# Batch 0 transposed on TensorE, its pairs scored in another order, split work in pieces, one plus three PSUM banks

## The chip, the cores and the metric

One core of a Trainium2 chip. The metric is device time in microseconds (us), median over runs. Most runs of one kernel lie within one per cent, but some lie higher: a run more than 1.5% above the fastest run of its kernel is called slow, and all comparisons here use the other, fast, runs. Ratios are the mean time of one kernel's fast runs over that of the other's fast runs of the same rounds on the same chip, so they are not quite the ratio of the medians that are quoted.

## The reference, cut to what matters

```python
def _attn_ref(q, k, v, proj):          # q, k, v: 4 batches, 8 heads, 768 rows, 64 columns
    q_bucket = bits_to_int(q @ proj > 0)      # 6 hash bits a row
    k_bucket = bits_to_int(k @ proj > 0)
    scores = where(q_bucket == k_bucket, scale * q @ k.T, -1e9)
    return softmax(scores) @ v

x = attention output as 3072 rows of 512
h = maximum(maximum(x @ w1, x @ w2), x @ w3)  # 512 -> 768
out = h @ w_out                               # 768 -> 512
```

## The kernel before

Heads are worked on in pairs, four pairs to a batch. To prepare a pair, q and k are split in two fp16 parts on VectorE (four instructions: `split_h` and `split_r` for each), transposed, and hashed: TensorE multiplies by the projection, VectorE compares and writes six rows of ±32768 under the 64 data rows, so that the score matmul masks by itself. A score unit is two score matmuls, one exp on ScalarE, and, two units later, six matmuls with v ("attend"). There are 192 units. When a half of a batch (four pairs) is done, its FFN is cut in atoms and strewn among the later units.

PSUM is the memory in which TensorE leaves its results; `bufs` is the number of buffers of a pool there. To evacuate a result is to copy it out, and until then its buffer is taken.

```python
sc_ps = ... bufs=2   # scores, two banks each
av_ps = ... bufs=2   # attend results
mm_ps = ... bufs=2   # all else: transposes, hash, mean of v, xT, FFN

def xbar(n, b, pr):  # the transpose by DMA
    nc.sync.dma_start_transpose(T[n, b, pr][:], S16[n, b, pr]...)

# batch 0: pairs 0 and 1 transposed on TensorE, 2 and 3 by DMA; splits partly on GpSimd
def prep(b, pr, s, lead, lag):          # batches 1 to 3; s is a unit
    at(s - lead, lambda: [load(n, b, pr, nc.gpsimd) for n in "qkv"])
    def split():
        operands(b, pr)
        for n in "qk":
            split_h(n, b, pr, nc.vector)
            split_r(n, b, pr)
            xbar(n, b, pr)
    at(s, split)
    at(s + 2, lambda: vcast(b, pr))
    at(s + lag, lambda: hash_half(b, pr, 0))
    at(s + lag + 1, lambda: hash_half(b, pr, 1))
    at(s + lag + 1, lambda: hash_rows(b, pr))
    at(s + lag + 2, lambda: meanv(b, pr))

for b in range(1, B):
    for pr in range(NP):
        if b == 1: prep(b, pr, 32 + 6 * pr, 10, 9)
        else:      prep(b, pr, 2 * (b - 1) * NUG + 14 + 10 * pr, 10, 10)

for u in range(N + LAG + 4):            # program order of every engine
    if u < N: score(u)
    if LAG <= u < N + LAG: attend(u - LAG)
    for fn in todo.pop(u, []): fn()
    ...                                 # FFN atoms, 0.64 us of them a unit
```

All engines take their instructions in this program order. (... marks cuts.)

The softmax here doesn't subtract the row's maximum and nothing guards it: scores larger than these inputs give would overflow.

## Time and profile before

| | before |
|---|---|
| time, median | 362.04 us (361.45 to 362.47, 3 runs) |
| TensorE (PE) busy | 292.0 us of a span of 359.8 |
| VectorE (DVE) busy | 202.2 us |
| ScalarE (ACT) busy | 197.3 us |
| mean granted TensorE clock | 0.915 |

The prediction below shows the lines. One slip in it has to be known first: its four dated exps are not units 41, 62, 150 and 191 but, counted from unit 0, units 45, 61, 152 and 191. These are units 41, 62 and 150 in the timeline of the kernel before (start, length, engine, line, operation, shapes, and in brackets the idle time before it and what ended it):

```profile
93.93 0.90 ACT L245 ACTIVATE AT<-sc,bias_t 128x768 f16<-128x768 f32 x1 [0.22 <-PE sc L241]
135.27 0.90 ACT L245 ACTIVATE AT<-sc,bias_t 128x768 f16<-128x768 f32 x1 [1.88 <-PE sc L241]
280.68 0.92 ACT L245 ACTIVATE AT<-sc,bias_t 128x768 f16<-128x768 f32 x1
```

### The profile page before, as it was taken

What the parts mean: (1) busy time and instruction counts of PE and PEld (TensorE: products, weight loads), DVE (VectorE), ACT (ScalarE), POOL (GpSimd) and SP (SyncE); (2) the same over time, 40 slices, a digit from 0 to 9 for tenths busy, and PEclk for the clock granted to TensorE, in tenths of its full rate; (3) what the DMA queues carried; (4) which work ended last, traced back from release to release, by engine and by line L of the source; (5) the groups of instructions that cost most, each with busy time, mean ns of one, the idle gap of its engine ahead of it and who ended that gap; (6) DMA issues with size and microseconds to landing.
All of it is one profiled execution on the core that took longest, in us unless ns stands there. A gap on an engine that the chain in (4) does not pass through costs nothing.

```text
span 359.8 us, 6801 instructions
## 1 busy us (share of the span) xinstructions
PE 292.0 (81%) x2752; PEld 178.2 (50%) x2752; DVE 202.2 (56%) x407; ACT 197.3 (55%) x257; POOL 80.5 (22%) x97
## 2 busy tenths in 40 slices
PE   1475709988769887987978896987978899999995
PEld 1253405655435454554644464554645466666552
DVE  2569504267578667577574655577575544444542
ACT  2346414866336355764664674764665587888221
POOL 1963220544160004404040012404010000010000
PEclk9999555589889899999898998999899999999999
DMA  7545998719955707666237108466224000200202
GB/s 257 189 112 101 132 127 136 262 26 197 214 120 165 118 3 189 192 146 177 46 89 161 58 3 219 162 147 174 49 39 108 31 1 2 89 2 1 89 0 87
DMA packets 58191, 39.76 MB, mean 111 GB/s; under 512 B 45360, under 2 KB 51888, under 8 KB 58160
## 3 DMA queue, kind: packets, MB, share of 16 engines
q1 hardware_dynamic: 49280, 20.06, 25.9%
q0 software_dynamic: 8432, 18.88, 21.4%
q8 instruction: 21, 0.34, 0.4%
q10 hardware_dynamic: 448, 0.40, 0.3%
q14 instruction: 10, 0.08, 0.1%
HBM read 25.17 MB, written 6.29 MB: 87 GB/s over the span
## 4 chain that ended last, share of the span: by engine, by line
PE 62%; DVE 24%; DMA 8%; issue 4%; ACT 1%; ACTq 0%; DVEq 0%
PE ps L306 24%; PE sc L241 15%; PE av L261 8%; PE po L318 8%; DMA kT<-ks 6%; DVE qs L148 4%; PE hps L174 4%; DVE ht L313 3%; DVE hb L179 3%; DVE ks L142 2%; DVE qT L183 2%; DVE qs L142 2%; DMA k<-in_k_dram 2%; DVE kT L183 2%; DVE ks L148 2%
## 5 line engine op out<-in xcount | busy, mean ns | idle before, releaser
L245 ACT ACTIVATE AT<-sc,bias_t 128x768 f16<-128x768 f32 x192 | 171.5, 903 | 103.4 <-PE sc L241 102.0
L306 PE MATMUL ps<-xT,w_sb 128*128 128x384 f16 x576 | 121.3, 337 | 14.0 <-DVE ht L313 12.2
L241 PE MATMUL sc<-qT,kT 70*128 70x384 f16 x384 | 104.3, 356 | 4.4 <-DVE qT L183 1.8
L313 DVE TENSOR_TENSOR ht<-ht,ps 128x384 f16<-128x384 f16 x96 | 52.6, 548 | 73.2 <-PE ps L306 72.0
L261 PEld LDWEIGHTS <-AT 128*128 128x128 f16 x1152 | 66.1, 103 | 31.4 <-issue 9.3
L282 POOL TENSOR_TENSOR xn<-t,rr 128x384 f16<-128x384 f32 x24 | 20.8, 868 | 242.4 <-PE sc L241 139.0
L306 PEld LDWEIGHTS <-w_sb 128*128 128x128 f16 x576 | 50.4, 100 | 46.8 <-issue 26.8
L261 PE MATMUL av<-vone,AT 128*128 128x65 f16 x1152 | 71.4, 200 | 0.0
L241 PEld LDWEIGHTS <-kT 70*128 70x128 f16 x384 | 37.5, 105 | 32.5 <-issue 8.1
L311 ACT CAST ht<-ps 128x384 f16<-128x384 f32 x48 | 22.8, 475 | 33.2 <-PE ps L306 33.2
L318 PE MATMUL po<-wout_sb,ht 128*128 128x512 f16 x144 | 36.4, 395 | 2.7 <-DVE hb L179 2.5
L179 DVE TENSOR_SCALAR hb<-hps 128x384 f16<-128x384 f32 x32 | 17.7, 554 | 34.3 <-PE hps L174 34.2
L174 PE MATMUL hps<-kT,PA 128*32 128x384 f16 x64 | 12.3, 377 | 15.7 <-DMA kT<-ks 10.1
L324 DVE COPY osb<-po 128x512 f32<-128x512 f32 x16 | 11.0, 690 | 21.3 <-PE po L318 21.3
L318 PEld LDWEIGHTS <-ht 128*128 128x128 f16 x144 | 13.3, 101 | 17.5 <-issue 6.3
L277 DVE TENSOR_TENSOR t<-av,mv 128x390 f32<-128x390 f32 x32 | 18.0, 561 | 6.1 <-PE av L261 5.8
L174 PE MATMUL hps<-qT,PA 128*32 128x384 f16 x64 | 13.2, 378 | 7.5 <-DVE xT L293 4.2
L292 PE MATMUL xps<-iden,xn 128*128 128x128 f16 x96 | 11.5, 234 | 9.2 <-DVE ht L313 9.2
L213 POOL CAST vone<-v 128x768 f16<-128x768 f32 x16 | 16.6, 1042 | 6.5 <-DMA v<-in_v_dram 6.3
L148 DVE SCALAR_TENSOR_TENSOR qs<-q,qs 128x768 f16<-128x768 f32 (+1 forms) x17 | 17.5, 1031 | 0.5
L148 DVE SCALAR_TENSOR_TENSOR ks<-k,ks 128x768 f16<-128x768 f32 (+1 forms) x17 | 17.0, 998 | 0.5
L174 PEld LDWEIGHTS <-PA 128*32 128x32 f16 x128 | 4.1, 95 | 25.9 <-issue 18.1
(47 smaller groups left out, 195.8 us busy)
## 6 DMA issues: line engine op xcount, KB each, us to landing
v<-in_v_dram POOLq DMA_DIRECT2D x16, 384.0 KB, 5.1
out_dram<-osb SPq DMA_DIRECT2D x24, 256.0 KB, 2.0
q<-in_q_dram POOLq DMA_DIRECT2D x12, 384.0 KB, 3.7
k<-in_k_dram POOLq DMA_DIRECT2D x12, 384.0 KB, 4.8
w_sb<-in_moe_w_dram POOLq DMA_DIRECT2D x6, 384.0 KB, 11.6
q<-in_q_dram SPq DMA_DIRECT2D x3, 384.0 KB, 5.8
k<-in_k_dram SPq DMA_DIRECT2D x3, 384.0 KB, 7.5
wout_sb<-in_moe_w_out_dram POOLq DMA_DIRECT2D x1, 768.0 KB, 15.2
```

What stands on the lines that cost most here:

```text
L148: nc.vector.scalar_tensor_tensor(out=s[:, a, D : 2 * D], in0=x32, scalar=QS, in1=s[:, a, 0:D], op0=AluOp.mult, op1=AluOp.subtract)
L174: nc.tensor.matmul(hps[32 * g : 32 * (g + 1), 0:HQ], w[:], t[:, a : a + CH, :], start=s, stop=not s)
L179: nc.vector.tensor_scalar(out=out, in0=hps[:, 0:HQ], scalar1=0.0, scalar2=0.5, op0=AluOp.is_gt, op1=AluOp.subtract)
L241: nc.tensor.matmul(sc[:, i, 0:HQ], kT[0:KR, hh * NCH + 2 * j + i, :], qT[0:KR, hh * NCH + hf * CH : hh * NCH + (hf + 1) * CH, :], start=Tr ...
L245: nc.scalar.activation(AT[:], sc[:, :, 0:HQ], ActFn.Exp, bias=bias_t[:], scale=EXP_SCALE)
L261: nc.tensor.matmul(av[:, o : o + D + 1], AT[:, i, c * P : (c + 1) * P], vones[b % 2][:, 2 * pr + hh, 2 * j + i, 0 : D + 1], start=first, s ...
L277: nc.vector.tensor_tensor(out=t[:, :, :, 0 : D + 1], in0=av[:, :, :, 0 : D + 1], in1=mvs[b, pr][:].unsqueeze(2).to_broadcast([P, 2, CH, D ...
L282: eng.tensor_tensor(out=xv, in0=t[:, :, :, 0:D], in1=rr[:].to_broadcast([P, 2, CH, D]), op=AluOp.mult)
L306: nc.tensor.matmul(ps[:, 0:HQ], w_sb[i][:, jc, fb * P : (fb + 1) * P], xT[:, jc, :], start=jc == 0, stop=jc == NJ - 1)
L311: nc.scalar.copy(ht[:], ps[:, 0:HQ])
L313: nc.vector.tensor_tensor(out=hts[fb][:], in0=hts[fb][:], in1=ps[:, 0:HQ], op=AluOp.max)
L318: nc.tensor.matmul(ps[:], hts[fb][:, c * P : (c + 1) * P], wout_sb[:, fb, :], start=fb == 0, stop=fb == NF - 1)
```

## The change

Its intent: take the DMA transposes out of batch 0, where TensorE stood for them, and let each pair's preparation hide behind more score work; cut the split block on VectorE into pieces, so that it holds up nothing for long; give the shared work three banks.

```diff
-    av_ps = ... bufs=2      mm_ps = ... bufs=2
+    av_ps = ... bufs=1      mm_ps = ... bufs=3
+    nc.scalar.dma_start(p32[:], proj[:, :])          # now ahead of the first k load
     load("q", 0, 0, nc.sync, (0, 1))
     load("k", 0, 0, nc.scalar, (0, 1))
 ...
-    units = [... for b in range(B) for hf in range(2) for pr in range(NP) ...]
+    blocks = [(0, hf, pr) for pr, hf in ((0, 0), (0, 1), (1, 0), (1, 1), (2, 0), (3, 0), (2, 1), (3, 1))]
+    blocks += [(b, hf, pr) for b in range(1, B) for hf in range(2) for pr in range(NP)]
 ...
+    def front(b, pr, s):                              # pairs 1 to 3 of batch 0
+        at(s, split_h q); at(s, split_r q); at(s + 1, split_h k); at(s + 1, split_r k)
+        ...  four TensorE transposes at s + 3 and s + 4, evacuated by VectorE
+        tail(b, pr, s + 5)
+    def tail(b, pr, s):                               # the hash work
+        at(s, hash_half 0); at(s + 1, hash_half 1); at(s + 2, rows of head 0); at(s + 3, rows of head 1)
 ...
     def prep(b, pr, s, lead, lag):
-        at(s, split)                                  # all four at once
+        for i, n in enumerate("qk"):
+            at(s + 2 * i, lambda n=n: split_h(n, b, pr, nc.vector))
+            at(s + 2 * i + 1, lambda n=n: split_r(n, b, pr))
+            at(s + 2 * i + 1, lambda n=n: xbar(n, b, pr))
+        at(s + 4, lambda: vcast(b, pr))
+        tail(b, pr, s + lag)
+        at(s + lag + 4, lambda: meanv(b, pr), 0.34)
-            if b == 1: prep(b, pr, 32 + 6 * pr, 10, 9)
-            else:      prep(b, pr, 2 * (b - 1) * NUG + 14 + 10 * pr, 10, 10)
+            if b == 1: prep(b, pr, 26 + 7 * pr, 7, 12)
+            else:      prep(b, pr, 2 * (b - 1) * NUG + 6 + 12 * pr, 10, 12)
 ...  FFN atoms begin at unit 41, at an even rate to the end; the first attend of a block goes behind them
```

Left out here: the loads of batch 0 move from the queues of GpSimd and ScalarE to that of SyncE, all but one; GpSimd loses its four splits of batch 0, and ScalarE three of its four evacuations.

More of the change, by code (lines that the diff above doesn't have):

```diff
@@ L60 @@
     sc_ps = ctx.enter_context(tc.tile_pool(name="sc_ps", bufs=2, space=bass.MemoryType.PSUM))
-    av_ps = ctx.enter_context(tc.tile_pool(name="av_ps", bufs=2, space=bass.MemoryType.PSUM))
-    mm_ps = ctx.enter_context(tc.tile_pool(name="mm_ps", bufs=2, space=bass.MemoryType.PSUM))
+    av_ps = ctx.enter_context(tc.tile_pool(name="av_ps", bufs=1, space=bass.MemoryType.PSUM))
+    mm_ps = ctx.enter_context(tc.tile_pool(name="mm_ps", bufs=3, space=bass.MemoryType.PSUM))
     ctx.enter_context(tc.manual_schedule())
@@ L78, in load @@
         eng.dma_start(r_[:, h0:h1, :], src.rearrange("h (p c) d -> p h (c d)", c=NCH))
+    p32 = konst.tile([D, NBITS], FP32, name="p32")
+    nc.scalar.dma_start(p32[:], proj[:, :])
     load("q", 0, 0, nc.sync, (0, 1))
     load("k", 0, 0, nc.scalar, (0, 1))
-    p32 = konst.tile([P, NBITS], FP32, name="p32")
-    nc.scalar.dma_start(p32[0:D, :], proj[:, :])
-    nc.scalar.dma_start(p32[D : 2 * D, :], proj[:, :])
     load("q", 0, 0, nc.sync, (1, 2))
-    load("k", 0, 0, nc.scalar, (1, 2))
-    load("q", 0, 1, nc.sync)
-    load("k", 0, 1, nc.sync)
-    load("v", 0, 0, nc.gpsimd)
+    load("k", 0, 0, nc.sync, (1, 2))
+    load("v", 0, 0, nc.sync)
+    for n in "qkv":
+        load(n, 0, 1, nc.sync)
     bias_t = konst.tile([P, 1], FP32, name="bias_t")
@@ L103 @@
         vones.append(t)
-    ph = konst.tile([P, NBITS], FP16, name="ph")
+    ph = konst.tile([D, NBITS], FP16, name="ph")
     PA = konst.tile([P, 32], FP16, name="PA")
@@ L109 @@
     nc.vector.memset(PB[:], 0.0)
-    pr32 = konst.tile([P, NBITS], FP32, name="pr32")
+    pr32 = konst.tile([D, NBITS], FP32, name="pr32")
     def make_p():
         nc.vector.tensor_copy(ph[:], p32[:])
-        nc.vector.tensor_scalar(out=PA[:, 0:NBITS], in0=ph[:], scalar1=1024.0, scalar2=None, op0=AluOp.mult)
         nc.vector.tensor_tensor(out=pr32[:], in0=p32[:], in1=ph[:], op=AluOp.subtract)
-        nc.vector.tensor_scalar(out=PB[:, 0:NBITS], in0=pr32[:], scalar1=1024.0, scalar2=None, op0=AluOp.mult)
+        for o in (0, D):
+            nc.vector.tensor_scalar(out=PA[o : o + D, 0:NBITS], in0=ph[:], scalar1=1024.0, scalar2=None,
+                                    op0=AluOp.mult)
+            nc.vector.tensor_scalar(out=PB[o : o + D, 0:NBITS], in0=pr32[:], scalar1=1024.0, scalar2=None,
+                                    op0=AluOp.mult)
     w_sb = [konst.tile([P, NJ, DF], FP16, name=f"w{i}_sb") for i in range(3)]
@@ L152, in xbar, with pe_T @@
         nc.sync.dma_start_transpose(T[n, b, pr][:], S16[n, b, pr][:].rearrange("p a d -> p (a d)"))
-    def pe_T(n, b, pr, hh, tag):
-        pool = av_ps if tag == "av" else mm_ps
-        ps = pool.tile([P, 512], FP32, tag=tag, name="tps")
+    def pe_T(n, b, pr, hh):
+        ps = mm_ps.tile([P, 512], FP32, tag="mm", name="tps")
         p16 = ps[:].bitcast(FP16)
@@ L192, in hash_half, with hash_rows @@
         hash_cmp(hbs[b, pr][:, half * HQ : (half + 1) * HQ], hps)
-    def hash_rows(b, pr):
-        hb = hbs.pop((b, pr))
+    def hash_rows(b, pr, heads=(0, 1)):
+        hb = hbs[b, pr]
         for g, (n, hh) in enumerate((("q", 0), ("k", 0), ("q", 1), ("k", 1))):
+            if hh not in heads:
+                continue
             dst = T[n, b, pr][D : D + NBITS, hh * NCH : (hh + 1) * NCH, :].rearrange("p a t -> p (a t)")
@@ L229 @@
     NU = NCH // 2
-    units = [(b, hf, pr, hh, j) for b in range(B) for hf in range(2) for pr in range(NP)
-             for hh in range(2) for j in range(NU)]
+    blocks = [(0, hf, pr) for pr, hf in ((0, 0), (0, 1), (1, 0), (1, 1), (2, 0), (3, 0), (2, 1), (3, 1))]
+    blocks += [(b, hf, pr) for b in range(1, B) for hf in range(2) for pr in range(NP)]
+    units = [(b, hf, pr, hh, j) for b, hf, pr in blocks for hh in range(2) for j in range(NU)]
     ATs = {}
@@ L265, in attend @@
             norm(b, hf, pr)
-            at(u + LAG + 3, lambda: x_T(b, hf, pr))
+            at(u + LAG + 3, lambda: x_T(b, hf, pr), 0.2)
     xTs = {}
@@ L285, in x_T @@
     def x_T(b, hf, pr):
-        if pr == 0:
+        if (b, hf) not in xTs:
             xTs[b, hf] = xp.tile([P, NJ, HQ], FP16, tag="xT", name="xT")
@@ L336, with at @@
     NUG = NP * 2 * NU
+    NUP = 2 * NU
     todo = {}
-    def at(step, fn):
-        todo.setdefault(step, []).append(fn)
+    def at(step, fn, pe=0.0):
+        todo.setdefault(step, []).append((pe, fn))
     operands(0, 0)
@@ L345 @@
     split_h("k", 0, 0, nc.scalar, (0, 1))
+    make_p()
     split_r("q", 0, 0, (0, 1))
     split_r("k", 0, 0, (0, 1))
+    pq = pe_T("q", 0, 0, 0)
+    pk = pe_T("k", 0, 0, 0)
+    evac_T(pq, "q", 0, 0, 0, nc.vector)
+    evac_T(pk, "k", 0, 0, 0, nc.scalar)
     split_h("q", 0, 0, nc.scalar, (1, 2))
     split_h("k", 0, 0, nc.scalar, (1, 2))
-    pq = pe_T("q", 0, 0, 0, "av")
-    pk = pe_T("k", 0, 0, 0, "mm")
-    evac_T(pq, "q", 0, 0, 0, nc.vector)
-    evac_T(pk, "k", 0, 0, 0, nc.scalar)
-    make_p()
@@ L355 @@
     split_r("q", 0, 0, (1, 2))
     hash_head(0, 0, 0)
-    split_r("k", 0, 0, (1, 2))
     vcast(0, 0)
-    for n in "qk":
-        load(n, 0, 2, nc.sync)
-    load("v", 0, 1, nc.gpsimd)
-    operands(0, 1)
-    split_h("q", 0, 1, nc.gpsimd)
-    split_h("k", 0, 1, nc.gpsimd)
     def first_b():
-        pq = pe_T("q", 0, 0, 1, "mm")
-        pk = pe_T("k", 0, 0, 1, "mm")
+        split_r("k", 0, 0, (1, 2))
+        pq = pe_T("q", 0, 0, 1)
+        pk = pe_T("k", 0, 0, 1)
         evac_T(pq, "q", 0, 0, 1, nc.vector)
-        evac_T(pk, "k", 0, 0, 1, nc.scalar)
-        hash_head(0, 0, 1)
@@ L373, in second @@
-    def second():
-        for n in "qk":
-            for hh in range(2):
-                ps = pe_T(n, 0, 1, hh, "mm")
-                evac_T(ps, n, 0, 1, hh, nc.vector if n == "q" else nc.scalar)
-    def third(pr):
-        operands(0, pr)
-        for n in "qk":
-            split_h(n, 0, pr, nc.gpsimd if pr == 2 else nc.vector)
-            split_r(n, 0, pr)
-            xbar(n, 0, pr)
-    at(0, first_b)
-    at(0, lambda: vcast(0, 1))
-    at(1, lambda: split_r("q", 0, 1))
-    at(1, lambda: split_r("k", 0, 1))
@@ L390 @@
-    at(2, second)
-    at(1, lambda: [load(n, 0, 3, nc.sync) for n in "qk"])
-    at(1, lambda: load("v", 0, 2, nc.gpsimd))
-    at(3, lambda: load("v", 0, 3, nc.gpsimd))
-    at(3, lambda: hash_half(0, 1, 0))
-    at(4, lambda: hash_half(0, 1, 1))
-    at(4, lambda: hash_rows(0, 1))
-    at(4, lambda: third(2))
-    at(5, lambda: vcast(0, 2))
-    at(6, lambda: meanv(0, 0))
-    at(6, lambda: load_w(0, 0))
-    at(7, lambda: load_w(1, 0))
-    at(8, lambda: meanv(0, 1))
-    at(8, lambda: third(3))
@@ L404 @@
-    at(9, lambda: vcast(0, 3))
-    at(9, lambda: load_w(2, 0))
-    at(10, lambda: hash_half(0, 2, 0))
-    at(11, lambda: hash_half(0, 2, 1))
-    at(11, lambda: hash_rows(0, 2))
-    at(12, lambda: load_w(0, 1))
-    at(13, lambda: load_w(1, 1))
-    at(14, lambda: load_w(2, 1))
-    at(14, lambda: meanv(0, 2))
-    at(15, lambda: hash_half(0, 3, 0))
-    at(16, lambda: hash_half(0, 3, 1))
-    at(16, lambda: hash_rows(0, 3))
-    at(18, lambda: meanv(0, 3))
-    at(18, lambda: nc.gpsimd.dma_start(wout_sb[:], moe_w_out.rearrange("(c p) m -> p c m", p=P)))
@@ L419, in prep @@
-    def prep(b, pr, s, lead, lag):
-        at(s - lead, lambda: [load(n, b, pr, nc.gpsimd) for n in "qkv"])
-        def split():
-            operands(b, pr)
-            for n in "qk":
-                split_h(n, b, pr, nc.vector)
-                split_r(n, b, pr)
-                xbar(n, b, pr)
-        at(s, split)
-        at(s + 2, lambda: vcast(b, pr))
-        at(s + lag, lambda: hash_half(b, pr, 0))
-        at(s + lag + 1, lambda: hash_half(b, pr, 1))
-        at(s + lag + 1, lambda: hash_rows(b, pr))
-        at(s + lag + 2, lambda: meanv(b, pr))
+        evac_T(pk, "k", 0, 0, 1, nc.vector)
@@ new lines, with load_pair, tr @@
+    at(0, first_b)
+    at(1, lambda: hash_head(0, 0, 1))
+    def load_pair(b, pr, eng):
+        for n in "qkv":
+            load(n, b, pr, eng)
+    def front(b, pr, s):
+        at(s, lambda: operands(b, pr))
+        at(s, lambda: split_h("q", b, pr, nc.vector))
+        at(s, lambda: split_r("q", b, pr))
+        at(s + 1, lambda: split_h("k", b, pr, nc.vector))
+        at(s + 1, lambda: split_r("k", b, pr))
+        def tr(n, hh):
+            evac_T(pe_T(n, b, pr, hh), n, b, pr, hh, nc.vector)
+        for i, (n, hh) in enumerate((("q", 0), ("k", 0), ("q", 1), ("k", 1))):
+            at(s + 3 + i // 2, lambda n=n, hh=hh: tr(n, hh), 0.34)
+        tail(b, pr, s + 5)
@@ new lines, in tail @@
+    def tail(b, pr, s):
+        at(s, lambda: hash_half(b, pr, 0), 0.34)
+        at(s + 1, lambda: hash_half(b, pr, 1), 0.34)
+        at(s + 2, lambda: hash_rows(b, pr, (0,)))
+        at(s + 3, lambda: hash_rows(b, pr, (1,)))
+    at(0, lambda: vcast(0, 1))
+    at(0, lambda: load_pair(0, 2, nc.sync))
+    front(0, 1, 2)
+    at(2, lambda: meanv(0, 0), 0.34)
+    at(5, lambda: load_pair(0, 3, nc.sync))
+    at(6, lambda: vcast(0, 2))
+    at(7, lambda: load_w(0, 0))
+    at(8, lambda: load_w(1, 0))
@@ new lines @@
+    at(9, lambda: load_w(2, 0))
+    front(0, 2, 11)
+    at(10, lambda: meanv(0, 1), 0.34)
+    at(15, lambda: vcast(0, 3))
+    front(0, 3, 19)
+    at(18, lambda: meanv(0, 2), 0.34)
+    for i in range(3):
+        at(16 + i, lambda i=i: load_w(i, 1))
+    at(26, lambda: meanv(0, 3), 0.34)
+    at(20, lambda: nc.gpsimd.dma_start(wout_sb[:], moe_w_out.rearrange("(c p) m -> p c m", p=P)))
+    def prep(b, pr, s, lead, lag):
+        at(s - lead, lambda: load_pair(b, pr, nc.gpsimd))
+        at(s, lambda: operands(b, pr))
+        for i, n in enumerate("qk"):
[5 more added lines that the diff above has]
+        at(s + lag + 4, lambda: meanv(b, pr), 0.34)
@@ L438 @@
             if b == 1:
-                prep(b, pr, 32 + 6 * pr, 10, 9)
+                prep(b, pr, 26 + 7 * pr, 7, 12)
             else:
-                prep(b, pr, 2 * (b - 1) * NUG + 14 + 10 * pr, 10, 10)
+                prep(b, pr, 2 * (b - 1) * NUG + 6 + 12 * pr, 10, 12)
     N = len(units)
+    begin = 6 * NUP + 5
+    rate = (7 * 24 * 0.64 + sum(c for st, l in todo.items() if begin <= st < N for c, _ in l)
+            + 0.2 * 28) / (N - begin)
     credit = 0.0
@@ L447 @@
             score(u)
-        if LAG <= u < N + LAG:
+        late = LAG <= u < N + LAG and (u - LAG) % NUP == 0
+        if LAG <= u < N + LAG and not late:
             attend(u - LAG)
-        for fn in todo.pop(u, []):
+        for pe, fn in todo.pop(u, []):
             fn()
-        if atoms:
-            credit += 0.64
+            if u >= begin:
+                credit -= pe
+        if u >= begin:
+            credit += rate
             while atoms and credit >= atoms[0][0] / 2:
@@ L457 @@
                 fn()
+        if late:
+            attend(u - LAG)
     for _, fn in atoms:
```

## The prediction

> **What bounds the kernel now.** I read first the page's row of slices, because the change touches mostly the first third.
>
> ```profile
> PE   1475709988769887987978896987978899999995
> DVE  2569504267578667577574655577575544444542
> PEclk9999555589889899999898998999899999999999
> ```
>
> A slice is 9 us. Slices 5 to 8 (36 to 73 us) hold a full stop of TensorE and half its clock. After slice 30 TensorE is full and VectorE (DVE) falls to 4: that is what the loop does undisturbed. Between, TensorE has holes. The work is a chain of 192 score units (two score matmuls, one exp, six attend matmuls), so I date everything by the exps. Counted from the first (unit 0), units 41, 62, 150 and 191 are these:
>
> ```profile
> 101.66 0.90 ACT L245 ACTIVATE AT<-sc,bias_t 128x768 f16<-128x768 f32 x1 [0.26 <-PE sc L241]
> 132.49 0.90 ACT L245 ACTIVATE AT<-sc,bias_t 128x768 f16<-128x768 f32 x1 [0.81 <-PE sc L241]
> 283.99 0.90 ACT L245 ACTIVATE AT<-sc,bias_t 128x768 f16<-128x768 f32 x1 [0.81 <-PE sc L241]
> 333.85 0.90 ACT L245 ACTIVATE AT<-sc,bias_t 128x768 f16<-128x768 f32 x1 [0.62 <-PE sc L241]
> ```
>
> From the last exp to the end (359.8) are 26.0 us: the FFN of the eighth half, with nothing beside it. Then the chain that ended last, first its piece in batch 0, then one in batch 2:
>
> ```profile
> 32.03 4.27 DMA kT<-ks
> 36.30 0.04 issue
> 36.34 0.52 PE hps L174 x5
> 36.86 17.69 DMA kT<-ks
> 54.55 0.04 issue
> ...
> 245.96 0.47 PE hps L174 x8
> 246.43 0.02 issue
> 246.45 0.56 DVE hb L179
> 247.01 0.73 DVE qs L142
> 247.74 0.02 issue
> 247.76 0.96 DVE qs L148
> 248.72 0.48 DVE ks L142
> 249.20 0.02 issue
> 249.23 0.96 DVE ks L148
> 250.19 0.28 DVE xT L293
> ```
>
> In batch 0 the path is 22 us of DMA transposes of pairs 2 and 3. In batch 2 it is the four split instructions of one pair, back to back on DVE, about 3.2 us; behind them stand the evacuations of hash, xT and FFN banks, so TensorE, with two banks for these, stands too (its idle before the hash matmul at 250.50 is 2.12 us). This recurs in every pair.
>
> Last, the granted clock by stretches:
>
> ```profile
> 54.00:73.00 19.00, 18.38 (x147) 11.47 (x147) 5.96 (x15) 12.32 (x15) 5.17 (x7) 0.50 0.77 190
> 160.00:240.00 80.00, 68.42 (x672) 41.85 (x671) 49.28 (x98) 46.78 (x62) 16.99 (x22) 0.94 0.45 118
> 300.00:330.00 30.00, 29.89 (x306) 19.26 (x305) 13.36 (x30) 24.06 (x32) 2.52 (x4) 1.00 0.07 27
> ```
>
> The first number after the stretch is its length, the next TensorE busy; the clock is third from the end. From 54 to 73 TensorE was busy 97% of the time and stayed at half clock.
>
> **What the Trainium skill says.** "TensorE: Matmul & The Clock Gate", Part 1, has TensorE at half clock after an idle window of some 3.4 us and at full clock after about as much busy time. The fall agrees (idle 32.7 to 36.3, clock 0.5 from then). The rise doesn't: 19 us of scores and attends did not bring it back; it came at 74, after the first two FFN groups. [...]The same page, Part 4, says that transposes do not lift the clock. Here 24 of them back to back (21.7 to 24.6) were followed by full clock at 26 (attends fell from 0.54 to 0.35), so I side with the trace, unsurely. "Perfetto Trace Analysis", Optimizing Scalar/DVE Operations, says that breaking up instructions that cause bubbles elsewhere may let work complete sooner; splitting the block of four does that. "SBUF — State Buffer", Who interferes with whom, has DVE's two-port and two-input instructions share a port with GpSimd. The trace agrees: the residual split takes 0.96 us alone and 1.47 beside GpSimd work.
>
> **The change part by part.**
> *Start.* Before, kT's evacuation sat on ScalarE behind a split that waited for the second k load (to 9.96), and the projection landed at 8.85; the hash began at 11.22 and the first exp at 14.7. Now the projection is loaded first and the evacuation stands ahead of that split. Splits from 4.1; six tiny projection operations at 0.15 (1 us) on DVE; two residuals of 0.56; 12 half-clock transposes (1.5 us); evacuation 0.8; hash 0.9; waiting behind one DVE residual, then comparison 0.56 and two rows of 0.3: first exp about 11.5. Gain 3 us.
> *Batch 0, DVE.* It loses GpSimd's help (four splits of 2.1 us there, 0.55 here) and ScalarE's (evacuations). A pair costs splits 2×0.55 + 2×0.96 = 3.0, four evacuations at 0.56 = 2.2, two comparisons 1.1, four rows at 0.36 = 1.4, a mean 0.3: 8.1. Up to unit 27: three pairs 24.3, the rest of pair 0 3.8, a mean 0.3, four norms at 0.75 and three xT at 0.35, 4: 32.4. ScalarE needs 27 × 0.91 = 24.6, so DVE sets the pace: 11.5 + 32.4 + 2 for hand-overs = unit 27 at 46. From 27 to 41 batch 1's pairs begin, one in 7 units at 5.9 (DMA transposes, no evacuation): 0.84 a unit, norms and xT 0.2: 1.04; ScalarE 0.91. I take 1.2: unit 41 at 63, against 101.7.
> *The order 0 0 1 1 2 3 2 3.* It gives pair 1 twelve units of lead instead of six, pairs 2 and 3 up to 24 and 30, so their preparation hides. The price: the first half is complete after six blocks instead of four, and FFN starts at unit 41 (before at about 29). The FFN of seven halves must then fit in 151 units.
> *Units 41 to 62.* TensorE: score and attend 0.51 (a unit with one FFN group takes 1.16, the group 0.65). FFN of a half 18 × 0.65 + 3 × 1.29 = 15.6, times 7 over 151: 0.72. xT 0.05, hash and mean (2×0.45 + 0.33)/7 = 0.18: 1.46. DVE: 0.84 + 0.2 + FFN (12 × 0.55 + 2 × 0.69)×7/151 = 0.37: 1.41. Two nearly full engines; I take 1.55: 33 us (before 30.8).
> *Units 62 to 150.* One pair in 12 units: TensorE 0.51 + 0.72 + 0.05 + 0.10 = 1.38, DVE 0.49 + 0.2 + 0.37 = 1.06. Splits come as four pieces over four units, and three banks take the evacuations, so the hole of about 4 us per pair should shrink to some 0.7: 1.44 a unit, 127 us (before 151.5, or 1.72).
> *Units 150 to 191.* No splits: 1.28, 41 units and a little more, 54 us (before 49.9 at the lower FFN share).
> *End.* Same work, 26 us.
> Sum: 63 + 33 + 127 + 54 + 26 = 303 us.
>
> **The rivals.**
> (1) The early part stays cold. With no FFN before unit 41 the clock may never rise: 41 units at 0.97 = 40, 14 transposes of a head at 0.73 = 10, hash 5, means 2.6, xT 1.8, in all 59.5 instead of 51.5 after 11.5: unit 41 at 71, total 311. For it speaks the stretch 54 to 73; against it the warm-up at 26 after transposes.
> (2) The single av bank. Each of 32 blocks must wait until DVE has read the last one (0.56) before its first attend; it was put behind the FFN of that step, so some 1.5 us cover it. If DVE is late by 1 us each time, 28 us come back: about 330. Against it: DVE needs 1.06 of 1.44 and its pieces are under 1 us.
> (3) DVE binds throughout 27 to 150 because GpSimd and DVE block each other (1.47 for 0.96): some 1.5 us a pair, 12 pairs, 18 us, total 320. Before, only a minority of splits after 140 us were slowed.
> (4) The gain of batch 0 is hidden, as the later FFN start leaves more work behind. It cannot eat it up: TensorE's total at full clock is about 250 us, 70% of today's time, so the holes decide.
> (5) Everything fits better than I allow: at 1.38 from 62 on and 1.45 before, 293.
>
> **Range and chances.** Of the 59 us gained, 39 are in before's stall of batch 0, 24 in the holes of units 62 to 150, and 6 are given back in the denser FFN. The first is nearly sure, as no DMA transpose is left in batch 0; the second depends on rivals 2 and 3. I predict 303 us, eight in ten between 291 and 319. Slower by over 2% would need both to fail: 1%; within 2%: 2%; faster: 97%.
>
> **What would show it.** Right if the first exp comes near 11.5; no wait for kT from a DMA is left before 60; unit 41's exp is near 63, unit 150's near 223, and 26 us follow the last; DVE's busy time is 205 to 212 us (before 202); the clock is 0.5 only before some 25 us, and the chain holds few split instructions after unit 62. Wrong if the clock stays 0.5 to the first FFN group (rival 1), if attends wait for DVE's norm over 0.3 us at each block (rival 2), or if the residual splits average over 1.2 us (rival 3).

## More of the kernel before

The experiments ran in groups on six chips; the kernel before, run again with each group, had medians of 359.6 to 363.0 us there, so a difference between two experiments that is given in us is good to a few us only.

With the right dates the engines' busy times in the four stages are, in us (length of the stage, then PE, weight loads, DVE, ACT and GpSimd busy, with instruction counts; at the end clock, DMA share and GB/s):

```profile
14.70:93.90 79.20, 57.09 (x507) 35.77 (x506) 40.06 (x74) 40.56 (x49) 30.71 (x34) 0.75 0.82 141
93.90:135.30 41.40, 34.48 (x345) 19.86 (x343) 28.96 (x60) 20.64 (x27) 7.17 (x8) 0.91 0.53 115
135.30:280.70 145.40, 124.43 (x1237) 76.72 (x1237) 90.67 (x179) 87.38 (x115) 30.57 (x40) 0.95 0.47 123
280.70:333.80 53.10, 51.13 (x530) 32.90 (x527) 24.85 (x55) 40.22 (x54) 4.99 (x6) 1.00 0.05 16
```

The length minus PE busy is TensorE's idle time: 22, 7, 21 and 2 us.

## The result, and the profile after

340.86 us (337.83 to 350.97, 4 runs) against 362.25: ratio 0.9385 (95% interval 0.9332 to 0.9437). It is faster, but by 21 us instead of 59, and outside the range of 291 to 319. The profiled run has a span of 336.0 us. Its slices of 8.4 us:

```profile
PE   1798696966998969799698987969989999999795
DVE  3688969652998585937549585593775544453452
PEclk9999878595999999989699995997999999999899
```

The full stop in slices 5 to 8 is gone; the holes further on are not. The timeline's exps of units 0, 41 and 62 and, in the fourth and fifth line, of units 149 with 150, and 191:

```profile
12.06 0.90 ACT L250 ACTIVATE AT<-sc,bias_t 128x768 f16<-128x768 f32 x1 [2.11 <-PE sc L246]
65.99 0.90 ACT L250 ACTIVATE AT<-sc,bias_t 128x768 f16<-128x768 f32 x1 [0.39 <-PE sc L246]
108.09 0.91 ACT L250 ACTIVATE AT<-sc,bias_t 128x768 f16<-128x768 f32 x1
255.15 1.70 ACT L250 ACTIVATE AT<-sc,bias_t 128x768 f16<-128x768 f32 x2
311.71 0.90 ACT L250 ACTIVATE AT<-sc,bias_t 128x768 f16<-128x768 f32 x1 [0.79 <-PE sc L246]
```

| stage, us | before | predicted | after | with both repairs found below |
|---|---|---|---|---|
| to the first exp | 14.7 | 11.5 | 12.1 | 12.2 |
| units 0 to 41 | 79.2 | 51.5 | 53.9 | 52.9 |
| units 41 to 62 | 41.3 | 33 | 42.1 | 32.8 |
| units 62 to 150 | 145.4 | 127 | 147.8 | 121.1 |
| units 150 to 191 | 53.2 | 54 | 55.8 | 55.8 |
| last exp to the end | 26.0 | 26 | 24.3 | 24.5 |
| span | 359.8 | 303 | 336.0 | 299.3 |

So four of the six stages came within 2.4 us of the prediction. Of the missing 33 us, 30 lie in two: 9 between units 41 and 62, 21 between 62 and 150. Busy times in those stages, same columns as before:

```profile
12.10:66.00 53.90, 45.90 (x520) 29.73 (x518) 44.38 (x87) 35.41 (x42) 22.58 (x28) 0.85 0.84 167
66.00:108.10 42.10, 33.67 (x333) 20.07 (x331) 28.64 (x59) 21.35 (x29) 9.73 (x12) 0.91 1.09 147
108.10:255.90 147.80, 131.00 (x1277) 80.31 (x1275) 96.82 (x183) 88.60 (x117) 28.13 (x36) 0.93 0.58 113
255.90:311.70 55.80, 55.80 (x560) 35.40 (x553) 27.25 (x58) 41.63 (x56) 4.99 (x6) 1.00 0.09 34
```

From 62 to 150 TensorE idles 147.80 − 131.00 = 16.8 us, and a mean clock of 0.93 means that 14% of the stage, some 20 us, ran at half clock, which costs about 10. 147.8 less these 27 is 121: what the prediction had as TensorE's pure need, 88 × 1.38. Where the idle time comes from shows the chain of waits in one pair's turn (start, length, what; pieces called "issue" of 0.05 us and less are left out):

```profile
156.86 0.30 DVE hb L181
157.21 1.43 DVE qs L151
158.64 0.47 DVE ht L318
159.14 0.40 DVE qT L185
159.57 0.57 DVE kT L185
160.17 1.06 DVE ks L145
161.26 0.04 DVE qT L185
161.30 0.33 issue
161.63 0.37 DVE kT L185
162.01 0.96 DVE ks L151
162.97 0.47 DVE ht L318
```

VectorE works without a break from 154.7 to 163.9. In the piece shown, 3.5 us are split pieces (qs, ks) of the next pair, about 2 us hash work, the comparison (hb) and the rows (qT, kT) of one pair, and 0.9 us maxima of the FFN (ht). Splits and hash work were put in the same four units, since the hash work follows its splits by 12 units and the splits of pairs follow each other by 12. TensorE ends up idle for 3.06 us (160.4 to 163.5), and right after it two score matmuls take 0.84 us instead of 0.49: the clock has halved. TensorE's timeline has both, with the wait for VectorE's ht:

```profile
159.24 0.49 PE L246 MATMUL sc<-qT,kT 70*128 70x384 f16 x2
163.49 1.44 PE L311 MATMUL ps<-xT,w_sb 128*128 128x384 f16 x4 [3.06 <-DVE ht L318]
164.72 0.84 PE L246 MATMUL sc<-qT,kT 70*128 70x384 f16 x2
```

From 41 to 62 the idle time is of another kind. From TensorE's timeline, hash matmuls of batch 1:

```profile
75.46 0.34 PE L176 MATMUL hps<-qT,PA 128*32 128x384 f16 x1 [3.29 <-DMA qT<-qs]
79.15 0.48 PE L176 MATMUL hps<-kT,PA 128*32 128x384 f16 x1 [3.35 <-DMA kT<-ks]
```

TensorE waits for DMA transposes, as before in batch 0, only now in batch 1.

### The profile page after: what moved, and what is told of

The parts are those of the page before. It is cut to its first block, busy times and chain, and to the rows that moved or that the text cites. A ratio compares the mean times of both kernels' runs of the same rounds, so it can differ in the third digit from the quotient of the medians.

```text
span 336.0 us, 6898 instructions
## 1 busy us (share of the span) xinstructions
PE 288.1 (86%) x2800; PEld 177.3 (53%) x2800; DVE 212.6 (63%) x424; ACT 195.0 (58%) x254; POOL 67.8 (20%) x89
## 3 DMA queue, kind: packets, MB, share of 16 engines
HBM read 25.17 MB, written 6.29 MB: 94 GB/s over the span
## 4 chain that ended last, share of the span: by engine, by line
PE 56%; DVE 24%; DMA 15%; issue 3%; ACT 1%; ACTq 0%; SPq 0%; DVEq 0%
PE ps L311 23%; PE sc L246 13%; DMA kT<-ks 13%; PE av L266 7%; PE po L323 6%; DVE qs L151 4%; DVE kT L185 3%; DVE ks L145 3%; DVE qT L185 3%; PE hps L176 3%; DVE ks L151 3%; DVE hb L181 2%; DVE ht L318 2%; PE tps L161 2%; DMA k<-in_k_dram 1%
## 5 line engine op out<-in xcount | busy, mean ns | idle before, releaser
L311 PE MATMUL ps<-xT,w_sb 128*128 128x384 f16 x576 | 118.6, 342 | 8.7 <-DVE ht L318 5.2
L246 PE MATMUL sc<-qT,kT 70*128 70x384 f16 x384 | 102.2, 349 | 2.2 <-DVE qT L185 1.2
L318 DVE TENSOR_TENSOR ht<-ht,ps 128x384 f16<-128x384 f16 x96 | 52.9, 551 | 52.0 <-PE ps L311 49.3
L266 PEld LDWEIGHTS <-AT 128*128 128x128 f16 x1152 | 64.4, 101 | 33.7 <-issue 10.5
L311 PEld LDWEIGHTS <-w_sb 128*128 128x128 f16 x576 | 53.1, 101 | 42.4 <-issue 18.1
L266 PE MATMUL av<-vone,AT 128*128 128x65 f16 x1152 | 70.2, 198 | 3.4 <-DVE t L282 2.7
L246 PEld LDWEIGHTS <-kT 70*128 70x128 f16 x384 | 34.6, 103 | 26.0 <-issue 10.0
L323 PE MATMUL po<-wout_sb,ht 128*128 128x512 f16 x144 | 35.0, 380 | 2.6 <-DVE ht L318 2.5
L151 DVE SCALAR_TENSOR_TENSOR qs<-q,qs 128x768 f16<-128x768 f32 (+1 forms) x17 | 19.4, 1142 | 2.0 <-ACT qs L143 1.7
L329 DVE COPY osb<-po 128x512 f32<-128x512 f32 x16 | 11.0, 690 | 12.1 <-PE po L323 12.0
L217 POOL CAST vone<-v 128x768 f16<-128x768 f32 x16 | 15.1, 941 | 14.8 <-DMA v<-in_v_dram 14.8
L297 PE MATMUL xps<-iden,xn 128*128 128x128 f16 x96 | 11.5, 233 | 6.8 <-DVE ht L318 4.2
L298 DVE COPY xT<-xps 128x384 f16<-128x384 f16 x32 | 11.3, 352 | 8.3 <-PE xps L297 7.8
```

The lines of the kernel that those rows point to most:

```text
L151: nc.vector.scalar_tensor_tensor(out=s[:, a, D : 2 * D], in0=x32, scalar=QS, in1=s[:, a, 0:D], op0=AluOp.mult, op1=AluOp.subtract)
L246: nc.tensor.matmul(sc[:, i, 0:HQ], kT[0:KR, hh * NCH + 2 * j + i, :], qT[0:KR, hh * NCH + hf * CH : hh * NCH + (hf + 1) * CH, :], start=Tr ...
L266: nc.tensor.matmul(av[:, o : o + D + 1], AT[:, i, c * P : (c + 1) * P], vones[b % 2][:, 2 * pr + hh, 2 * j + i, 0 : D + 1], start=first, s ...
L311: nc.tensor.matmul(ps[:, 0:HQ], w_sb[i][:, jc, fb * P : (fb + 1) * P], xT[:, jc, :], start=jc == 0, stop=jc == NJ - 1)
L318: nc.vector.tensor_tensor(out=hts[fb][:], in0=hts[fb][:], in1=ps[:, 0:HQ], op=AluOp.max)
L323: nc.tensor.matmul(ps[:], hts[fb][:, c * P : (c + 1) * P], wout_sb[:, fb, :], start=fb == 0, stop=fb == NF - 1)
```

## The experiments

Theory A: from unit 62 on, hash work and splits in the same units pile up on VectorE, make a hole of about 3 us in TensorE, and the hole halves the clock. Rival B: the bank split binds. Rival C: VectorE has simply too much work. Theory D, for units 41 to 62: the hash waits for DMA transposes that are slowed by the loads of batch 1.

### 1. The hash work 18 units after its splits instead of 12

```diff
-                prep(b, pr, 2 * (b - 1) * NUG + 6 + 12 * pr, 10, 12)
+                prep(b, pr, 2 * (b - 1) * NUG + 6 + 12 * pr, 10, 18)
```

> Changed kernel, but in batches 2 and 3 the hash work of a pair comes 18 units after its splits instead of 12, so that it no longer falls into the four units in which the next pair is split. Theory A (hash and split work piled on VectorE in the same four units makes the hole of each pair, and the hole then halves TensorE's clock): units 62 to 150 fall from 148 us to about 128, clock there 0.98 or more, total 318 to 326. Rival B (the bank split 1 + 3 is what binds) and rival C (VectorE is simply too loaded on average): total stays at 335 to 343.

Measured: 313.12 us, ratio 0.8727 to before. Its busy times from unit 62 to 150:

```profile
110.10:231.20 121.10, 121.02 (x1273) 76.29 (x1271) 91.08 (x183) 88.75 (x117) 31.68 (x36) 1.00 0.65 139
```

Length and PE busy are the same number but for 0.08, and the clock is 1.00. One changed number gives 27 us, and all of them here. VectorE's work is less too (91 against 97 us): the mean residual split of this stage takes 1.03 us instead of 1.20, as two of the 14 take about 1.45 us where it was seven. Most of them still run beside GpSimd work in this trace, so what made the slow ones rarer is not shown. Theory A holds; B and C, which had expected no gain, fall.

### 2. The banks of before in the changed kernel

```diff
-    av_ps = ... bufs=1      mm_ps = ... bufs=3
+    av_ps = ... bufs=2      mm_ps = ... bufs=2
```

> Changed kernel with the PSUM banks of before: two av banks and two shared ones. If the single av bank costs (rival 2 of the prediction), it gets faster, to about 325 to 332. If the third shared bank helps, as the change intends, slower by 5 to 12 us: 345 to 352. Theory A alone says that the pile on VectorE is far longer than one bank covers: within 5 us of 340.

Measured: 357.29 us, two of four runs slow; the fast two are 350.95 and 355.35 (ratio 0.9827, 95% interval 0.9602 to 1.0053), on average 12 above the changed kernel's median. So the third shared bank gains more than the single av bank costs; as both numbers change, the run doesn't part them. The mean over fast runs, 353.2, is just above what the second line expected; the profile is of a slow run.

### 3. The four splits in one unit again

```diff
-            at(s + 2 * i, split_h n);  at(s + 2 * i + 1, split_r n, xbar n)
+            at(s, split_h n);          at(s, split_r n, xbar n)
```

> Changed kernel with the four split instructions of a pair in batches 1 to 3 issued in one unit again, as before, all else unchanged. If cutting the block into pieces is worth what the prediction gave it (most of 24 us), 355 to 365. Theory A: the pieces changed little, because they are still in the units of the hash work: 338 to 347.

Measured: 324.53 us, ratio 0.903: 16 us faster than the changed kernel, which neither line had expected. From unit 62 to 150:

```profile
106.60:243.00 136.40, 122.91 (x1277) 76.17 (x1275) 93.92 (x183) 88.75 (x118) 27.51 (x36) 1.00 0.48 117
```

Idle is 13.5 us instead of 16.8, not much less, but the clock is 1.00 instead of 0.93. In one block the splits make up to two holes of 1.4 us or less a pair, and the clock fell after none of them. Interleaved with hash work they make holes of up to 3.1 us: the clock fell during or after three of the four above 2.4 us (not after 2.75 us at 120.4), and with two of 1.5 and 1.4 us close together (200.7 and 203.0). So longer or crowded holes cost clock here; a fixed length at which they do can't be read from these runs. The splits of a block also take less time (0.96 us for a residual split on average, 1.20 in pieces). So at this distance the pieces did harm.

### 4. The kernel before with 15 units of distance instead of 10

```diff
-                prep(b, pr, 2 * (b - 1) * NUG + 14 + 10 * pr, 10, 10)
+                prep(b, pr, 2 * (b - 1) * NUG + 14 + 10 * pr, 10, 15)
```

> Kernel before with the hash work of batches 2 and 3 at 15 units after the splits instead of 10, which was its period too. Theory A: the same pile was in the kernel before, so it gains 8 to 16 us there too, to 346 to 354. Rivals B and C: unchanged, 360 to 364.

Measured: 357.31 us, ratio 0.9962 (0.9844 to 1.008): no difference that can be told. The kernel before has the same coincidence, 10 and 10, but parting the two gains it nothing: its idle from 62 to 150 goes from 20.5 to 18.9 us, by the gaps between matmuls; most of what is left are waits for VectorE's ht and xT. So with two shared banks the splits in one block stop TensorE also when the hash work is elsewhere. Theory A in the form "the pile alone makes the hole" was too wide.

### 5. and 6. Distance 18 with the block, and with two plus two banks

> Hash work moved to 18 units as in the first run, and the four splits of a pair in one unit again. If the distance alone fills the holes, 311 to 316 like the first run. If the pieces matter once the hash work is out of their way, as the change intended, a hole of about 1 us per pair stays (VectorE 3 us in one block against three banks): 318 to 325.

Measured: 310.98 us, ratio 0.8695.

> Hash work at 18 units, pieces kept, but two av and two shared banks. Theory A with enough slack: no pile, so two shared banks do, 313 to 320. If the third bank is needed for the normal course (each piece of VectorE work holds an evacuation up by about 1 us), 322 to 335, with holes of about 1 us spread over the units.

Measured: 332.84 us, ratio 0.9273.

With these, the cells of the changed kernel are (median, and in brackets the stage from unit 62 to 150):

| | distance 12 | distance 18 |
|---|---|---|
| pieces, 1 + 3 banks | 340.9 (147.8) | 313.1 (121.1) |
| block, 1 + 3 banks | 324.5 (136.4) | 311.0 (125.5) |
| pieces, 2 + 2 banks | 357.3 (slow profile) | 332.8 (130.3) |

The pieces are worth 4 us in this stage once the distance is right, and cost 11 where it isn't. The third bank is worth 9 us there at the right distance, and another 12 between units 41 and 62 (41.4 us against 53.1). In the fifth run the total is still a little lower than in the first, because blocks in batch 1 start the DMA transposes earlier (units 41 to 62 in 37.6 us against 41.4; number 9 tests this alone).

### 7. The kernel before with the new banks alone

```diff
-    av_ps = ... bufs=2      mm_ps = ... bufs=2
+    av_ps = ... bufs=1      mm_ps = ... bufs=3
```

> Kernel before with only the bank change: one av bank, three shared ones. The second run put the third bank at 16 us in the changed kernel; if that holds here, 342 to 352. If the single av bank costs without the late placing of the first attend (rival 2 of the prediction), 362 to 375.

Measured: 340.17 us, ratio 0.9478. Two numbers give the time that the whole change gives. From unit 62 to 150 this takes 9.7 us off (135.7 against 145.4), and the rest comes from every other stage but the first:

```profile
127.90:263.60 135.70, 118.52 (x1241) 73.93 (x1244) 91.25 (x183) 87.55 (x114) 31.02 (x40) 0.99 0.51 132
```

The single av bank cost 6.0 us of waits in all, seven of them, without the late placing of the first attend; in the changed kernel, with it, there are two, 2.7 us.

### 8. Pairs 2 and 3 of batch 0 transposed by DMA again, in the changed kernel

```diff
-        four TensorE transposes and evacuations;  tail(b, pr, s + 5)
+        if pr >= 2: at(s, xbar q); at(s + 1, xbar k);  tail(b, pr, s + 8)
```

> Changed kernel with pairs 2 and 3 of batch 0 transposed by DMA again, with three units more until their hash work. If taking the transposes from the DMA queues is what gained the 28 us up to unit 41, this gives back 8 to 20 us there: total 348 to 360. If the new order's lead would have hidden them anyway, unit 41 stays at 64 to 69 us and the total at 336 to 345.

(`tail` is the hash work, here three units later.) Measured: 339.34 us, ratio 0.9454: no difference to the changed kernel in all. To unit 41 and then to unit 62:

```profile
12.40:75.90 63.50, 52.25 (x472) 31.55 (x470) 39.29 (x79) 36.40 (x42) 21.96 (x28) 0.65 0.86 187
75.90:107.90 32.00, 30.61 (x332) 19.05 (x330) 28.45 (x59) 21.39 (x28) 9.71 (x12) 1.00 0.87 151
```

Unit 41 comes 10 us later, as the first line had it, but unit 62 comes at 107.9, where the changed kernel has 108.1. What the TensorE transposes had gained was waited away again in batch 1, for transposes that were late anyway.

### 9. The first run's kernel with batch 1's splits in a block

> The first run's kernel (hash work at 18 units in batches 2 and 3, splits in pieces there), with the splits of batch 1 in one block, so that its DMA transposes start up to three units earlier. If what is left from unit 41 to 62 is lateness of those transposes, this stage falls from 41.4 us to 37 to 39 as with blocks everywhere, and the rest stays: total 307 to 311. If not: 313.

Measured: 309.05 us, ratio 0.8598; units 41 to 62 in 37.4 us. Earlier transposes help, as theory D says.

### 10. The first run's kernel with pairs 0 and 1 of batch 1 transposed on TensorE

```diff
-                at(s + 2 * i + 1, lambda n=n: xbar(n, b, pr))
+                if b == 1 and pr < 2:  two TensorE transposes with evacuation at s + 2 * i + 2 and + 3
+                else:                  at(s + 2 * i + 1, lambda n=n: xbar(n, b, pr))
```

> The first run's kernel with pairs 0 and 1 of batch 1 transposed on TensorE, as batch 0 is. Theory D (from unit 41 to 62 the hash waits for DMA transposes that share the DMA engines with the loads of batch 1): no wait for a DMA there, idle of the stage 8 us to under 3, stage 33 to 37 us, total 305 to 310. Rival (VectorE, with 2.2 us more of evacuation per pair, binds there): stage 40 or more, total 312 to 318.

Measured: 308.29 us, ratio 0.8513; the stage takes 32.7 us, its idle time is 1.9, but unit 41 comes 3.5 us later. Without the DMA transposes the wait is gone, so the first half of theory D holds; whether the loads slow the transposes is the next run's question.

### 11. Batch 1's loads on the queue of the transposes

```diff
-        at(s - lead, lambda: load_pair(b, pr, nc.gpsimd))
+        at(s - lead, lambda: load_pair(b, pr, nc.sync if b == 1 else nc.gpsimd))
```

> The first run's kernel with batch 1's loads on the queue that also carries the transposes, so that loads and transposes come one after the other instead of side by side. If running side by side is what stretches the transposes, the waits for kT and qT fall and the total goes to 306 to 311. If it is the volume, 311 to 316. If the transposes now stand behind loads that wait for a buffer, worse: 316 to 330.

Measured: 301.66 us (299.64 to 304.02), ratio 0.8385: the fastest kernel but for number 15, which is its equal. In the changed kernel the issuing engine is held by transposes of batch 1 like this:

```profile
61.07 12.79 SPq L155 DMA_TRANSPOSE kT<-ks  x1
73.95 4.53 SPq L155 DMA_TRANSPOSE qT<-qs  x1
78.57 8.51 SPq L155 DMA_TRANSPOSE kT<-ks  x1
```

and in this kernel, for the same three:

```profile
61.97 2.45 SPq L155 DMA_TRANSPOSE kT<-ks  x1
...
67.80 1.44 SPq L155 DMA_TRANSPOSE qT<-qs  x1
70.47 2.53 SPq L155 DMA_TRANSPOSE kT<-ks  x1
```

TensorE no longer waits for them. From issue to landing these three take 4.4, 3.9 and 6.9 us here, against 18.0, 16.7 and 13.4 in the changed kernel, where nine loads of 384 KB, issued at 56.7 to 61.8 and at 74.2 to 75.7 us, land among them. So the loads do slow the transposes, and theory D holds as a whole. From unit 41 to 62 and to 150:

```profile
65.10:97.90 32.80, 30.59 (x329) 18.92 (x328) 29.46 (x60) 21.54 (x30) 10.04 (x12) 1.00 0.87 166
97.90:219.00 121.10, 121.02 (x1272) 76.30 (x1271) 91.19 (x184) 88.64 (x118) 31.38 (x36) 1.00 0.70 139
```

### 12. The kernel before with new banks and 15 units of distance

> Kernel before with the new banks (340 alone) and the hash work at 15 units after the splits (357 alone, no gain). If the distance can only pay once a third shared bank lets TensorE run on while VectorE splits: units 62 to 150 fall from 136 us to 122 to 128, total 326 to 334. If the distance pays only with the splits in pieces: 337 to 342.

Measured: 334.93 us, but one run of four lay at 328.1 and made the others (334.7 to 336.0) slow ones, so the total is not settled. The profile, of one of those, has 130.9 us from 62 to 150 against 135.7 with the banks alone: about half of the expected gain. If fast runs have it too, which no profile shows, the distance pays something once the bank is there, less than with the splits in pieces.

### 13. The loads' queue alone, distance 12 kept

> Changed kernel with nothing but batch 1's loads on the transposes' queue. If the two faults are independent, the stage from unit 41 to 62 falls from 42 to 32 to 34 us and units 62 to 150 stay at 145 to 150: total 326 to 333. If the holes of the later batches came from transposes and not from the pile on VectorE, they shrink too: under 320.

Measured: 328.91 us, ratio 0.905. Units 41 to 62 take 32.6 us, 62 to 150 still 150.8:

```profile
99.50:250.30 150.80, 133.07 (x1277) 80.97 (x1275) 96.81 (x184) 88.82 (x117) 27.77 (x36) 0.92 0.60 112
```

The two faults are independent: 12 us for the queue, 28 for the distance, and 39 together (340.9 to 301.7).

### 14. Number 11 with pairs 2 and 3 of batch 0 by DMA

> The best kernel so far (301.7: hash work at 18 units, batch 1's loads on the transposes' queue) with pairs 2 and 3 of batch 0 transposed by DMA again. In the changed kernel this cost 10 us up to unit 41 and gave them all back by unit 62. If that was because unit 62 hung on batch 1's transposes anyway, the cost now shows: 306 to 314. If transposes on TensorE are worth nothing there, 299 to 304.

Measured: 308.3 us, ratio 0.8498. Now that nothing takes it back, transposing these pairs on TensorE is worth 6.6 us (6.8 against number 15, of the same rounds). Up to unit 41:

```profile
11.80:72.60 60.80, 52.02 (x472) 31.39 (x470) 38.08 (x79) 36.40 (x42) 13.87 (x17) 0.65 0.93 200
```

TensorE is busy for 52.0 us, with fewer instructions than the 45.2 us of number 11's stage: the clock is 0.65 instead of 0.87. It is idle for 8.8 us against 7.8. So most of the 7.9 us between the two stages is clock and not idle time; what keeps the clock down is not shown.

### 15. Number 11 with the projection loaded after the first k load

> The best kernel so far with the projection's load after the first k load on its queue instead of ahead of it, all else unchanged. If loading it first matters, the first exp comes 1 us or more later than 12 us, and the total is 1 to 2 us up. If something else sets the first exp (the splits and transposes), the first exp stays within 0.5 us, the total at 300 to 304.

Measured: 301.49 us, ratio 0.8327; first exp at 11.4 us. Loading the projection first gains nothing; in the changed kernel the first k split starts at 6.29 us, before at 4.41 and here at 3.98, as k's load stands behind the projection's there.

### 16. Number 11 with batch 1's loads on ScalarE's queue

> The best kernel (301.7) with batch 1's loads on ScalarE's queue: again beside the transposes, as in the changed kernel, but no longer issued by GpSimd. If running side by side is what stretches the transposes, the waits for qT and kT come back: 308 to 315. If it was GpSimd's way of issuing them, 299 to 305.

Measured: 303.97 us, ratio 0.8475. Within the second line, and no hash waited for a DMA from unit 41 to 62 (31.0 us). But the trace doesn't bear out that running side by side is harmless. The second pair's transposes, with these loads beside them, took 11.5 and 10.6 us from issue to landing, against 6.2 and 4.4 in number 11 and 17.8 and 18.0 in the changed kernel; the second of them held the issuing engine like this:

```profile
60.91 5.72 SPq L155 DMA_TRANSPOSE kT<-ks  x1
```

The conditions differ as well: the last pair's loads start at 66.1 us here and at 60.4 in the changed kernel, and unit 41 comes at 69.8 us, 4.6 later than in number 11, which gives the transposes more time. So running side by side does stretch them; whether issuing from GpSimd adds to it, this run can't tell.

### 17. Number 11 with 8 units of distance

> The best kernel with the hash work of batches 2 and 3 at 8 units after the splits instead of 18: again apart from the next pair's splits, but with four units less than the changed kernel gives the DMA transposes. If the coincidence with the splits makes the holes, none come back: 300 to 306. If what 18 units helped was the time for the transposes to land, the holes return, now with waits for qT or kT: 320 or more.

Measured: 344.95 us, ratio 0.9601. The holes came back, with this wait, 98 to 240 us:

```profile
PE hps L176 <- DMA kT<-ks: 21.5, 7, 5.0
```

Seven waits, 21.5 us in all, and two more for qT, 7.3 us. Eight units are too few for the transposes; there is a lower bound to the distance as well. The run could not tell whether 18 units helped by parting the two or by leaving the transposes time.

### 18. Number 11 with 24 units, two periods, for pairs 0 to 2

> The best kernel with the hash work of pairs 0 to 2 of batches 2 and 3 at 24 units, two periods, after their splits: five times it falls into the units of another pair's splits again, while the DMA transposes have even more time than at 18. If the coincidence makes the holes, five of them of some 3 to 4 us come back: 312 to 322, with waits for VectorE and none for a DMA. If the time to land was what 18 units bought: 299 to 305.

Measured: 314.94 us, two fast runs of 313.44 and 311.14; ratio 0.8615 (95% interval 0.8541 to 0.869) against 0.8385 (0.8326 to 0.8444) for number 11. More time for the transposes, and some 10 us slower by the fast runs, within the first line: five coincidences, some 2 us each. No wait for a transpose from unit 62 to 150 is in its trace. The profile is of a slow run (316.4), so its sizes are not quoted. With number 1 this settles that it is the coincidence.

## Why the prediction was wrong, point by point

- *Start*: right in size (11.5, measured 12.1). The reason was half right: the projection's place gives nothing (number 15). That moving the evacuation ahead of the split did it is what the two traces suggest (kT's evacuation starts at 10.39 us before and at 8.32 after); no run isolates it.
- *Batch 0*: right in size (51.5, measured 53.9), with VectorE 82% and TensorE 85% busy. Its gain is 93.9 − 66.0 = 28 us, not 39, as the dates of before were misread. And "the first is nearly sure, as no DMA transpose is left in batch 0" gave the transposes too much: putting two pairs back on DMA costs 8 to 10 us of the 25 in this stage (numbers 14 and 8), and in the total nothing in the changed kernel and 6.6 us in the repaired one. What the new order alone gives stays open: with the old one the later pairs would be scored before their rows are written, so it was not run.
- *Units 41 to 62*: the step failed that took 33 us from TensorE's and VectorE's work alone. Batch 1 is still transposed by DMA, and the hash waited for it. The sum itself was right: 32.8 us with the loads issued elsewhere. "No wait for kT from a DMA is left before 60" was literally true; the waits came at 72 and 76.
- *Units 62 to 150*: the step failed that says "the hole of about 4 us per pair should shrink to some 0.7" (with the right dates its own working gives 3.3 and not 4). It left out what else VectorE does in those four units. Distance and period were both 12, so the pieces were laid between the hash work of another pair. VectorE then works up to 9 us in a row, TensorE stands for up to 3 us, and the clock halves: 16.8 us of idle and about 10 of clock. Undone by one number, the stage took 121.1 us (predicted 127).
- *Units 150 to 191, and the end*: 54 and 26, measured 55.8 and 24.3; right.
- *Rival 1* (cold start): only in part; the clock was 0.85 up to unit 41, not 0.5 throughout. (The trace's record of the clock begins at 18.9 us, and what lies before counts as full; two score matmuls took 0.83 us until then, as at half clock. With that the estimate is 0.79.)
- *Rival 2* (the single av bank): wrong, and the other way round: the bank change is worth 22 us to the kernel before, by itself (number 7), and 12 to the changed one (2). The prediction's sum gave it no line of its own.
- *Rival 3* (VectorE and GpSimd block each other): the mechanism is there, 1.20 us for a residual split in this stage (seven at about 1.45 us beside GpSimd work, seven at 0.96 alone), but VectorE was busy for 96.8 of 147.8 us only. It lengthened the pile and did not bind.

The predicted time was nearly met, 301.7 against 303, by the kernel with both repairs. The prediction had summed what each engine needs, and not what the schedule puts into the same units.

## What to carry to other kernels

When work is laid out in a fixed period, look at the distance between the parts of one item modulo that period: a distance equal to it puts the tail of one item on top of the head of the next, on the same in-order engine; nor may it be so short that the transfers in between land late (number 17). Cutting a long instruction block into pieces helped here only where the gaps between the pieces are free; among other work it can turn two short stalls into one long one, and a long one may cost clock as well. And before crediting a gain to a removed wait, ask what the next stage hangs on: here batch 1's transposes took it all back until they were mended.

## What the Trainium skill lacked or had wrong

- "TensorE: Matmul & The Clock Gate": Part 1 has the full clock back after a few microseconds of busy TensorE; in the kernel before TensorE stayed at 0.50 for 19 us at 18.38 us busy. It has the clock fall after an idle window of some 3.4 us; in the changed kernel it fell during an idle time of 1.90 us (38.5 to 40.4) and after one of 2.35 (53.1 to 55.5). The prediction's "idle 32.7 to 36.3" isn't one window either, but 1.86 and 1.45 us around a hash matmul. Part 4 says that transposes don't lift the clock; with four more heads of batch 0 transposed on TensorE the clock up to unit 41 was 0.87 instead of 0.65 (numbers 11 and 14). What exactly lifts it stays open: in the changed kernel it rose at about 19 us, just ahead of pair 1's transposes, after 3.7 us in which only scores, attends and a mean of v ran.
- "DMA: Bandwidth & Descriptors", Issuing engines are not separate DMA queues, says that DMAs of all issuing engines interleave on the same DMA engines and that issuing from several only saves the sequencer's time. The interleaving agrees: transposes beside loads took up to 18.0 us to land, and 3.9 to 6.9 where the loads stood in the same queue. What it lacks is that the queue decides what runs beside what: with the same twelve loads the kernel took 313.1 us from GpSimd, 304.0 from ScalarE and 301.7 from SyncE (the last two are not told apart by their intervals).
- No page has that work on one in-order engine can pile up because its distance equals the period: 147.8 us against 121.1 in one stage.
